# A decode-attention kernel on one core: the last item's keys and values with reversed rows, and 512 columns of its values in loads of their own

## The chip, the cores and the metric

The kernel runs on one core of a Trainium2 chip. The metric is device time in microseconds of one execution; the median of three runs before the change is 695.87 us (695.85 to 696.24). A profiled execution of the same kernel, 695.97 us, is the source of every row shown.

## The reference

Two branches are mixed by a gate. Branch A is one decode step of attention with a cache of 4096 keys, 2 batches, 32 heads of 128; branch B is a feed-forward layer with SiLU.

```
q = (x @ wq) per head
scores = einsum("bhqd,bhkd->bhqk", q, k_cache) * Dh**-0.5
p = softmax(scores); o = einsum("bhqk,bhkd->bhqd", p, v_cache)
a = o.reshape(B, 1, H*Dh) @ wo
b = silu(x @ w1) @ w2
g = sigmoid((x * gate_w).sum(-1)); out = g * a + (1 - g) * b
```

Everything is float32. Keys and values are 134 MB each, and each of their bytes is used once. The softmax sums over all keys of a head, so the order in which a head's keys stand does not matter as long as its values stand in the same order.

## The kernel before

Work goes by items. An item is a group of four heads of one batch; there are 16 (`N`), numbered 0 to 15. Its keys are a run of 2,097,152 numbers that lie one after the other in the cache, and so are its values. `run_of` cuts such a run into 128 rows, one for each partition, of 16384 numbers (64 KB). Head q of the four fills partitions 32q to 32q+31, and a partition holds 128 keys of 128 numbers.

Three slabs of 64 KB per partition lie in SBUF. Keys go to slab `a` (even items) or `b` (odd items) by `load_k`, values to slab `v` by `load_v`; only the values of item 15 go to slab `a`, which the keys of item 14 have left by then. After the last values the weights of the output, `wo`, come in five loads (`load_wo`), the first ones into slab `v`, the last three into slab `b`.

For an item, POOL (L707) and DVE (L713) multiply the keys by the query in place, DVE adds them up to scores (L723) and finds the largest (L731 to L741), ACT takes the exponentials into `pz` (L752), PE multiplies them with the values (L799, 64 matmuls), and a short chain of DVE and PE turns the result into a column of `oP`. At the end PE multiplies `oP` by `wo`: three groups in halves (L590), a merge (L602, L607), and the last group in quarters (L620). The copy of L929 and one small store end the kernel.

All loads are issued by SP, in the order of the program, each when its slab is free, and run on one DMA queue. The loop over items issues the values of item i right after the products of item i, and the keys of item i+2 after the scores of item i. The keys of item 15 therefore stand behind the values of item 13, the values of items 14 and 15 one behind the other, and `wo` behind these. A small planner (`Flow`) notes for every operation which earlier ones it depends on, and turns that into semaphore waits; `dma` takes a semaphore and the value it will have reached (`count`), and `users` lists the operations that last wrote or read a slab. PE's loop covers the items 0 to 14; the matmuls of item 15 (L799) wait for the load of its values by name.

Of the kernel before, what the change touches and what calls it, by code (L numbers as in the profile page):

```python
# [189 lines left out]
def gated_decode(nc, x, kc, vc, wq, wo, w1, w2, gate, out):  # L190
    P = 128
    B, H, SK, DH = kc.shape
# [12 lines left out]
    SLAB = C * DH  # L205
# [11 lines left out]
    N = len(items)  # L217
# [3 lines left out]
    f = Flow(nc)  # L221
# [11 lines left out]
    slab = {n: slabs[:, k * SLAB : (k + 1) * SLAB] for k, n in enumerate("vba")}  # L233

    def part(n, *ks):
        return [f"{n}.{k}" for k in (ks or range(8))]
# [59 lines left out]

    def run_of(flat, i):
        hq, b = items[i]
        return flat[b, hq].rearrange("(p c) -> p c", p=P)

    def load_k(i):
        n = kslab(i)
        f.dma("SP", slab[n], run_of(kflat, i), writes=part(n), count=(h_k[i % 2], 16 * (i // 2 + 1)))
# [3 lines left out]
    def load_v(i):  # L307
        src = run_of(vflat, i)
        if i < N - 1:
            v_load[i] = f.dma("SP", slab["v"], src, writes=part("v"), signal=h_v if i < LOOPED else None)  # L310
            return
        f.dma("SP", slab["a"], src, writes=part("a"))

    def load_wo(g):

# [24 lines left out]
        writes=part("v", 0),  # L340
# [10 lines left out]
        writes=["ident"],  # L351
# [12 lines left out]
        writes=["block"],  # L364
# [7 lines left out]
        writes=["fold"],  # L372
# [5 lines left out]
        writes=["sel"],  # L378
# [5 lines left out]
        writes=["half"],  # L384
# [10 lines left out]
        writes=["pick"],  # L395
# [5 lines left out]
        writes=["own"],  # L401
# [5 lines left out]
        writes=["side"],  # L407
# [7 lines left out]
        writes=["spread"],  # L415
# [5 lines left out]
        writes=["mask"],  # L421
    )
    f.op("DVE", lambda: V.memset(join, 0.0), writes=["join"])
    for e in range(2):
# [7 lines left out]
            writes=["join"],  # L432
        )
        for t in (at, at + 32):
# [4 lines left out]
                writes=["join"],  # L439
# [11 lines left out]
        writes=["xt"],  # L451
# [6 lines left out]
        writes=["gx"],  # L458
# [7 lines left out]
    for b in range(B):  # L466
        for j in range(J):
# [13 lines left out]
                writes=[f"hsum{b}"],  # L481
            )

    def mm_hr():
# [19 lines left out]
        writes=["ps_o"],  # L504
# [7 lines left out]
        writes=["g"],  # L512
# [5 lines left out]
        writes=["gc"],  # L518
# [7 lines left out]
    for e in range(2):  # L526
# [4 lines left out]
            writes=[f"spaced{e}"],  # L531
# [9 lines left out]
        writes=["he"],  # L541
    )
    for e in range(2):
# [6 lines left out]
            writes=[f"seq{e}"],  # L550
# [125 lines left out]
    for u in range(2):  # L676
        for b in range(B):
# [8 lines left out]
                writes=[f"qall{u}{b}"],  # L686
            )

    load_v(0)
    load_k(1)  # L690
    query(0)
# [195 lines left out]
    for i in range(N + 1):  # L887
# [13 lines left out]
        if 1 <= i < N:  # L901
            load_v(i)
# [86 lines left out]
```

## Time and profile before

| | |
|---|---|
| median of three runs | 695.87 us |
| profiled execution | 695.97 us |
| its span (first to last instruction) | 694.6 us |
| busy share of DVE, POOL, PE | 73%, 38%, 31% |
| data moved | 298.32 MB, 429 GB/s over the span |
| share of the 16 DMA engines, data queue | 99.3% |
| one load of keys or values | 8.39 MB |

The page gives the busy time of each engine, the span in 40 slices with the share of the 16 DMA engines, the DMA queues, and the chain of work that ended last. A stretch is a piece of the span for which the same numbers are given; its DMA share counts each packet's duration in the stretch in which the packet began, so in a very short stretch it can pass 1. "SPq" is an issue of a transfer, not its movement.

### The profile page before, as it was taken

How to read it: one execution, taken by the hardware profiler on the slowest of the kernel's cores; microseconds unless marked ns; L12 is line 12 of the kernel's file. 1: busy time of each engine (PE TensorE's matmuls, PEld its weight loads, DVE VectorE, ACT ScalarE, POOL GpSimd, SP SyncE). 2: the span in 40 equal slices, each digit the busy share in tenths (PEclk: the TensorE clock that was granted, in tenths of full speed). 3: DMA queues.
4: the chain of work that ended last, by engine and by line, in shares of the span. 5: the costliest groups of instructions: out<-in, count | busy, mean ns of one | idle time of the engine just before them, and what ended most of it. 6: DMA issues, size and time to landing. Idle time of an engine off the chain costs nothing. (4 is left out here: it accounts for less than half of the span.)

```text
span 694.6 us, 3767 instructions
## 1 busy us (share of the span) xinstructions
PE 211.9 (31%) x1440; PEld 70.2 (10%) x1440; DVE 506.9 (73%) x269; ACT 40.0 (6%) x152; POOL 265.6 (38%) x26
## 2 busy tenths in 40 slices
PE   0073033151331506060412305060513215060556
PEld 0031010010110101010100101010101001010112
DVE  3910958898989697886959596986959595977901
ACT  0001010101010101010010101010000101010100
POOL 1000908190827090815335180906244270907100
PEclk9997556565565657566575757575665757575779
DMA  9999999999999999999999999999999999999997
GB/s 383 429 426 473 426 423 427 423 464 434 423 430 423 442 457 423 423 430 434 464 423 423 430 426 468 426 423 430 423 468 430 423 430 423 453 445 423 430 417 309
DMA packets 6051, 298.32 MB, mean 429 GB/s; under 512 B 652, under 2 KB 672, under 8 KB 928
## 3 DMA queue, kind: packets, MB, share of 16 engines
q1 hardware_dynamic: 6048, 298.27, 99.3%
q8 instruction: 3, 0.05, 0.0%
HBM read 298.26 MB, written 0.01 MB: 429 GB/s over the span
## 5 line engine op out<-in xcount | busy, mean ns | idle before, releaser
L707 POOL TENSOR_TENSOR slabs<-slabs,qsb 128x7680 f32<-128x7680 f32 x16 | 262.4, 16400 | 378.9 <-DMA slabs<-in_A_k_cache_dram 330.8
L723 DVE TENSOR_REDUCE s<-slabs 128x68 f32<-128x8704 f32 (+1 forms) x32 | 276.3, 8677 | 0.0
L799 PE MATMUL ps<-slabs,pz 128*32 128x512 f32 x1024 | 147.2, 739 | 337.1 <-PEq L156 328.9
L713 DVE TENSOR_TENSOR slabs<-slabs,ps 128x8704 f32<-128x8704 f32 x16 | 147.5, 9221 | 103.8 <-DMA slabs<-in_A_k_cache_dram 103.2
L799 PEld LDWEIGHTS ps<-slabs,pz 128*32 128x32 f32 x1024 | 39.7, 132 | 433.5 <-issue 425.2
L752 ACT ACTIVATE pz<-s,nb 32x128 f32<-32x128 f32 x64 | 25.5, 398 | 545.8 <-PE ps L799 353.2
L837 PE MATMUL ps<-osb,pick 128*128 128x512 f32 x32 | 21.1, 747 | 60.9 <-PEq L156 59.9
L821 DVE SCALAR_TENSOR_TENSOR osb<-ps,rg,own 128x512 f32<-128x512 f32 x16 | 12.0, 750 | 23.4 <-PE ps L799 23.1
L852 DVE TENSOR_REDUCE row<-ps 64x128 f32<-64x512 f32 x16 | 10.9, 682 | 24.0 <-PE ps L837 24.0
L773 PE MATMUL ps<-rs,fold 128*128 128x1 f32 x32 | 6.2, 262 | 40.9 <-PEq L156 40.8
L475 DVE SCALAR_TENSOR_TENSOR slabs<-slabs 128x1728 f32<-128x1728 f32 x8 | 16.2, 2019 | 0.3
L487 PE MATMUL ps<-slabs,xz_col 128*32 128x432 f32 x16 | 3.1, 927 | 33.4 <-DVE slabs L475 33.4
L837 PEld LDWEIGHTS ps<-osb,pick 128*128 128x128 f32 x32 | 5.4, 211 | 75.0 <-issue 73.1
L752 ACT ACTIVATION_READ_ACCUMULATOR pz<-s,nb 32x1 f32 x64 | 11.8, 184 | 0.0
L773 PEld LDWEIGHTS ps<-rs,fold 128*128 128x128 f32 x32 | 6.2, 226 | 54.2 <-issue 53.3
L859 DVE STREAM_TRANSPOSE ps<-row 64x256 f32<-64x256 f32 x16 | 10.3, 643 | 0.6
L567 PE MATMUL ps<-slabs,seq 128*32 128x320 f32 x54 | 9.2, 496 | 3.7 <-DVE seq L546 3.7
L642 PE MATMUL ps<-slabs,xz_col 128*32 128x512 f32 x80 | 9.8, 593 | 0.0
L652 PE MATMUL ps<-qall,spread 128*128 (+1 forms) x32 | 9.0, 371 | 0.8 <-ACT qall L680 0.8
L929 DVE COPY slabs<-ps 128x160 f32<-128x160 f32 x1 | 0.3, 324 | 11.9 <-PE ps L620 11.9
L590 PE MATMUL ps<-slabs,oP_xs 128*32 128x320 f32 x96 | 6.9, 434 | 2.4 <-DMA slabs<-in_A_wo_dram 2.4
L652 PEld LDWEIGHTS ps<-qall,spread 128*128 128x128 f32 x32 | 6.1, 236 | 1.7 <-ACT qall L680 1.7
(63 smaller groups left out, 69.8 us busy)
## 6 DMA issues: line engine op xcount, KB each, us to landing
slabs<-in_A_wq_dram SPq DMA_DIRECT2D x1, 10240.0 KB, 44.5
slabs<-in_B_w_dram SPq DMA_DIRECT2D x2, 4320.0 KB, 16.9
slabs<-in_A_wo_dram SPq DMA_DIRECT2D x1, 5120.0 KB, 22.7
slabs<-in_A_wo_dram SPq DMA_DIRECT2D x1, 2560.0 KB, 28.3
slabs<-in_A_wo_dram SPq DMA_DIRECT2D x1, 1600.0 KB, 31.9
slabs<-in_A_wo_dram SPq DMA_DIRECT2D x1, 640.0 KB, 32.9
slabs<-in_A_wo_dram SPq DMA_DIRECT2D x1, 320.0 KB, 33.2
slabs<-in_A_k_cache_dram SPq DMA_DIRECT2D x16, 47.9
```

The lines of the kernel that those rows point to most:

```text
L475: lambda b=b, j=j, at=at: V.scalar_tensor_tensor(hsum[:, b, :], w1t[:, j, :], at, hsum[:, b, :], op0=ALU.mult, op1=ALU.add)
L652: return T_.matmul(ps_q[:, :DH], spread, qall.rearrange("p n b u d -> p (n b u) d")[:, i, :], start=True, stop=True,)
L707: lambda: G_.tensor_mul(k[:, CV:, :], k[:, CV:, :], qsb[:, None, :].to_broadcast([P, C - CV, DH])),
L713: lambda: V.tensor_mul(k[:, :CV, :], k[:, :CV, :], ps_q[:, None, :DH].to_broadcast([P, CV, DH])),
L723: lambda c0=c0, c1=c1: V.reduce_sum(Ss[i % 2][:, c0:c1], k[:, c0:c1, :], axis=AX.X),
L752: last = S_.activation(pz[lo:hi, :, 4 * q : 4 * q + 4], s[lo:hi].rearrange("p (g c) -> p g c", c=4), AF.Exp, bias=nb[lo:hi], scale=SCALE, ...
L773: lambda *_: T_.matmul(ps_t[:, :1], fold.rearrange("p a q c -> p (a q c)"), rs, start=True, stop=True),
L799: last = T_.matmul(ps_v[32 * q : 32 * q + 32, :], pz[:, gr, :], v[:, gr, :], start=(gr < 4), stop=(gr >= NG - 4),)
L821: lambda: V.scalar_tensor_tensor(osb, ps_v.rearrange("p (c d) -> p c d", d=DH), rg, own[:, :, None].to_broadcast([P, 4, DH]), op0=ALU.mult ...
L837: lambda *_: T_.matmul(ps_o, pick, osb.rearrange("p c d -> p (c d)"), start=True, stop=True),
L852: lambda: V.reduce_sum(row, ps_o[:64].rearrange("p (c d) -> p d c", d=DH), axis=AX.X),
L859: lambda: V.transpose(oT.rearrange("p n (e i) -> p n e i", e=2), twice),
```

## The change

For item 15 alone, `run_of` no longer gives 128 rows but 16 blocks of 8 rows, the rows of each block in reversed order: partition 8a+m gets row 8a+7-m. Both its keys and its values go through `run_of`, so their rows stay together, and a block lies within one head. The rows are as long as before.

The values of item 15 are loaded in three transfers in place of one. The first brings columns 0 to 15871 to all 128 partitions. The second brings the last 512 columns (2 KB per partition) to partitions 0 to 95, which are blocks 0 to 11; the third brings these columns to partitions 96 to 127, blocks 12 to 15. All three wait for the same users of slab `a` and count up one new semaphore, to 16, 32 and 48; the matmuls of item 15 wait for 48. Bytes, arithmetic and the order of the issues are otherwise unchanged.

```diff
     def run_of(flat, i):
         hq, b = items[i]
+        if i == N - 1:
+            return flat[b, hq].rearrange("(a m c) -> a m c", a=16, m=8)[:, ::-1, :]
         return flat[b, hq].rearrange("(p c) -> p c", p=P)
 
@@ load_v
-        f.dma("SP", slab["a"], src, writes=part("a"))
+        to, cut, after, last = slab["a"], SLAB - 4 * DH, f.users(part("a")), f.sem("last_values")
+        f.dma("SP", to[:, :cut], src[:, :, :cut], after=after, count=(last, 16))
+        f.dma("SP", to[:96, cut:], src[:12, :, cut:], after=after, count=(last, 32))
+        f.dma("SP", to[96:, cut:], src[12:, :, cut:], writes=part("a"), after=after, count=(last, 48))
```

## The prediction

> **What bounds the kernel now.** I read the head of the page first: busy time of the engines, the two DMA rows of the 40 slices, and the queues.
>
> ```profile
> span 694.6 us, 3767 instructions
> ...
> PE 211.9 (31%) x1440; PEld 70.2 (10%) x1440; DVE 506.9 (73%) x269; ACT 40.0 (6%) x152; POOL 265.6 (38%) x26
> ...
> DMA  9999999999999999999999999999999999999997
> GB/s 383 429 426 473 426 423 427 423 464 434 423 430 423 442 457 423 423 430 434 464 423 423 430 426 468 426 423 430 423 468 430 423 430 423 453 445 423 430 417 309
> DMA packets 6051, 298.32 MB, mean 429 GB/s; under 512 B 652, under 2 KB 672, under 8 KB 928
> ...
> q1 hardware_dynamic: 6048, 298.27, 99.3%
> q8 instruction: 3, 0.05, 0.0%
> ```
>
> One queue keeps all 16 DMA engines busy for 99.3% of the span, while no compute engine passes 73%. The kernel is a stream of 298 MB; whatever makes the engines move a byte more slowly is paid in full, and a transfer can be hidden behind nothing. The timeline's rows of the last items show the order of that stream.
>
> ```profile
> 580.65 0.33 SPq L72 DMA_DIRECT2D slabs<-in_A_v_cache_dram  x1
> ...
> 581.02 0.43 SPq L72 DMA_DIRECT2D slabs<-in_A_k_cache_dram  x1
> ...
> 590.21 9.22 DVE L713 TENSOR_TENSOR slabs<-slabs,ps 128x8704 f32<-128x8704 f32 x1 [5.53 <-DMA slabs<-in_A_k_cache_dram]
> ...
> 618.77 0.80 SPq L72 DMA_DIRECT2D slabs<-in_A_v_cache_dram  x2
> ...
> 628.86 9.22 DVE L713 TENSOR_TENSOR slabs<-slabs,ps 128x8704 f32<-128x8704 f32 x1 [6.07 <-DMA slabs<-in_A_k_cache_dram]
> ...
> 656.84 2.31 SPq L72 DMA_DIRECT2D slabs<-in_A_wo_dram  x5
> ...
> 667.50 9.16 PE L799 MATMUL ps<-slabs,pz 128*32 128x512 f32 x64 [8.15 <-DMA slabs<-in_A_v_cache_dram]
> ```
>
> The keys of item 15 (the last) are issued at 581.02, behind the values of item 13, and are used from 628.86. The values of items 14 and 15 are issued together at 618.77; those of item 15 are used from 667.50. So the stream after 609.5 is: keys 15, values 14, values 15, then the five loads of wo. The stretches of 19.3 us give their rates (third number from the end the granted clock, then DMA share, GB/s).
>
> ```profile
> 590.20:609.50 19.30, 0.00 (x0) 0.00 (x0) 19.16 (x5) 0.00 (x0) 16.39 (x1) 0.50 1.00 435
> 609.50:628.80 19.30, 10.86 (x70) 3.28 (x70) 10.92 (x10) 2.22 (x9) 0.00 (x0) 0.77 1.00 435
> 628.80:648.10 19.30, 0.00 (x0) 0.00 (x0) 19.09 (x5) 0.00 (x0) 16.39 (x1) 0.50 1.00 435
> 648.10:667.40 19.30, 10.04 (x68) 2.99 (x68) 11.30 (x12) 1.96 (x8) 0.00 (x0) 0.77 0.98 426
> 667.40:679.50 12.10, 10.29 (x66) 2.49 (x66) 1.44 (x3) 0.00 (x0) 0.00 (x0) 0.82 1.00 432
> ```
>
> Every load of 8.39 MB takes 19.3 us: 435 GB/s, or 27.2 GB/s for each of 16 engines, so an engine's eight rows of 64 KB take 2.41 us each. The chain that ended last, in order of time, shows the end.
>
> ```profile
> 657.78 31.89 DMA slabs<-in_A_wo_dram
> 689.67 0.14 issue
> 689.80 2.16 PE ps L620 x56
> 691.97 0.02 issue
> 691.99 0.51 PE ps L620 x8
> 692.50 0.02 issue
> 692.52 0.32 DVE slabs L929
> ```
>
> The landings of wo end the kernel, with 2.9 us of matmuls, copy and issue behind the third-last of them. How the 16 engines finish is in quarter-microsecond stretches.
>
> ```profile
> 689.75:690.00 0.25, 0.20 (x8) 0.22 (x12) 0.00 (x0) 0.00 (x0) 0.00 (x0) 1.00 0.84 338
> 690.00:690.25 0.25, 0.25 (x16) 0.24 (x12) 0.00 (x0) 0.00 (x0) 0.00 (x0) 1.00 0.39 154
> ...
> 691.50:691.75 0.25, 0.25 (x16) 0.12 (x4) 0.00 (x0) 0.00 (x0) 0.00 (x0) 1.00 0.00 0
> 690.25:691.50 1.25, 1.25 (x43) 1.01 (x36) 0.00 (x0) 0.00 (x0) 0.00 (x0) 1.00 0.18 74
> ```
>
> Most engines have moved their last byte by 690.25, but from there to 691.50 a share of 0.18, or 0.18 x 16 = 2.9 engines, is still at work. Three engines are some 1.3 us late. The trace does not name them. The queue of instructions moved three packets; one falls in this stretch of 1 us:
>
> ```profile
> q1 hardware_dynamic: 34, 0.42, 99.4%
> q8 instruction: 1, 0.02, 5.9%
> ```
>
> 5.9% of 16 engine-microseconds is 0.95 us on one engine. Three packets, three late engines: I take it that each packet set one engine back for the rest of the run.
>
> **The change, part by part.** Part 1, fewer bytes for the last engines. Which transfer runs on how many engines shows in the packets under 512 B, which hold each engine's completion write: 652 = 40 x 16 + 3 x 4. Forty transfers have 128 rows; the three others (x, gate, output) have a slowest dimension of four on one side, though x fills eight partitions. So I expect the load of twelve blocks on 12 engines and that of four blocks on 4. The 512 columns are 512/16384 = 1/32 of the load, 19.3/32 = 0.60 us per engine. The last four engines get none of them (-0.60), the first four get two shares (+0.60 and some packet overhead, say +0.7), the middle eight stay. If the late three are among the last four, the end moves from 691.9 by -0.6; the first four, 1.3 us ahead, stay covered. If they are elsewhere it moves by 0 to +0.7. The tail of PE follows the landings either way.
>
> The Trainium skill, page "DMA: Bandwidth & Descriptors", section "Why a DMA increments its semaphore by 16 and not by 1", says that the engine count is the largest number up to 16 that divides the slowest dimensions of both sides, on the lowest-numbered engines; the 652 agree.
>
> Part 2, three issues for one. The row of 618.77 gives 0.80 us for two, so 0.8 more on SP. Nothing is behind them on SP until wo at 656.84, 38 us later, and the queue is fed 29 us ahead (618.77 against 648.1). Cost nothing; without that cover 0.8. The matmuls of L799 wait for all three, as for the one before. The two small loads' 128 extra packets lie in the shares above.
>
> Part 3, the source in sixteen blocks of eight rows, read backwards. This applies to all of keys 15 and values 15, 16.5 MB. No load of the trace has this form, so I bound it. From below: a row stays one piece of 64 KB (62 KB for the values), and the rate stays 435 GB/s as in the stretches above: 0. A gain has a reason against it, since each engine already streams without a gap (share 1.00). From above: the sixteen engines need not meet the partitions as they do now. If engine e takes block e, neighbouring partitions in one engine, two engines can want the same way into SBUF at a time, and two that share a way get half the rate each. Then keys 15 take 2 x 19.3, +19.3; values 15 without the 512 columns 2 x 18.7, +18.7; together +38.0. The nearest row to such sharing is the packet of instructions: 16 KB beside a data stream on one engine took 0.95 us, where 27.2 GB/s would give 0.60.
>
> Which end? The 128-row form lets the hardware deal out single rows, the new one only blocks of eight; what the old dealing bought is then lost, and the engines of a pair start these loads within 1.3 us of each other, against 9.7 us for four rows, so they would meet nearly all the time. I take the upper end, though the choice is close.
>
> The Trainium skill, page "SBUF — State Buffer", section "Door 1: The DMA port swizzle", gives each of 16 ports two groups of four partitions 32 apart and 27.2 GB/s, and "DMA: Bandwidth & Descriptors", section "The descriptor swizzle", says that a 128-partition transfer deals the partitions so that each engine has one port. By these rules blocks 0 and 4 would both be in port 0, then both in port 2, and half the ports would idle: the sum would be +38. If the swizzle held for the new form too, it would be part 1 alone. No row here shows which.
>
> Sum: 695.97 (the profiled execution; its span of 694.6 and 1.4 around it) + 19.3 + 18.7 + 0 for part 1 (between -0.6 and +1.2, since the pieces may share too) = 734.0. The median of the runs is 0.1 below the profiled one: **733.9**. All that waits on the keys of item 15 (L713, L707, the exponentials, the issue of wo) moves 19.3 with them; wo, issued 10.6 us ahead of need now (656.84 against 667.4), would be issued 29 us ahead, so no new gap opens.
>
> **The rivals.** *Same rate, late engines relieved* (the other side): the layout costs nothing and part 1 alone remains. For it: 64 KB rows, share 1.00, 16 engines on both forms. Against: the dealing out must change. Time 695.87 - 0.6 = 695.3 where the late engines are the last four, up to 696.6 where one is among the first; it decides where the keys of item 15 still land by 629. This holds the case that the small loads spread over all 16 engines after all: 695.9.
>
> *Sharing only once*: the engines of a pair drift apart by four rows in the keys of item 15, because one is served first, and then no longer meet. That costs four rows, 4 x 2.41 = 9.7 us once: 705.6; partial overlap fills the space up to 733.9. For it: engines run independently, as the late ones show. Against: a lateness of 1.3 us persists here and does not grow.
>
> *A layout that gains over 0.2%*: it needs 1.4 us, more than the 1.3 that all three late engines have. Against it everything above.
>
> **How the numbers follow.** Half rate in both loads 0.44, sharing in part 0.14, same rate 0.40, gain 0.02. 0.2% (1.4 us) is what a measurement of this kernel can tell from no change; the same-rate rival lies wholly inside it. So slower 0.58, same 0.40, faster 0.02. Predicted 733.9; its own range with partial sharing is 704 to 736. Since the cases of both signs hold nearly all the chance, the range runs from 694.9 to 736.
>
> **What would show it.** In the changed kernel's stretches, 609.5 to 648.1 at about 217 GB/s and the values of item 15 likewise, with the values of item 14 between at 435; L713's last wait longer by 19.3 us; wo landing some 38 us later, the tail behind it as now. Packets: 128 + 16 more, 668 under 512 B if the small loads run on 12 and 4 engines (652 - 16 + 32). Wrong would be: keys 15 landing by 629 (then the same-rate rival, and the tail from 690.25 to 691.50 shortens by 0.6), or a slow first load and a fast second (sharing once).

## The result and the profile after

The median of six runs is 741.45 us (740.52 to 742.49), against 696.02 us before (695.81 to 696.72): a ratio of 1.0652, interval 1.0638 to 1.0665. That is 45.4 us slower. The forecast was 733.9, with a range up to 736: the direction and the mechanism came out, the size did not. Lines of the code have moved by five, so L718 answers to L713 of before, L804 to L799, L625 to L620 and L934 to L929.

The head of the page of the changed kernel:

```profile
span 740.2 us, 3769 instructions
...
DMA  9999999999999999999999999999999999899897
GB/s 385 443 441 439 414 447 432 425 446 429 429 446 418 439 446 414 443 443 418 443 439 418 446 439 411 450 443 411 446 446 411 446 397 220 184 393 259 185 313 324
DMA packets 6195, 298.32 MB, mean 403 GB/s; under 512 B 668, under 2 KB 688, under 8 KB 1072
...
q1 hardware_dynamic: 6192, 298.27, 99.4%
q8 instruction: 3, 0.05, 0.0%
```

The same 298.32 MB, and the DMA engines are as busy as before (99.4%). What has changed is the row of GB/s: two dents near the end, to about half. An engine with a slow packet counts as busy, so the share (99.3% before) does not show the loss. The packets under 512 B are 668, which is 652 - 16 + 32: this fits pieces on 12 and 4 engines, as forecast.

The timeline of the changed kernel, at the uses of the last loads:

```profile
612.53 8.49 PE L804 MATMUL ps<-slabs,pz 128*32 128x512 f32 x64 [29.86 <-PEq L156]
...
652.49 9.22 DVE L718 TENSOR_TENSOR slabs<-slabs,ps 128x8704 f32<-128x8704 f32 x1 [27.38 <-DMA slabs<-in_A_k_cache_dram]
...
674.91 9.72 PE L804 MATMUL ps<-slabs,pz 128*32 128x512 f32 x64 [50.94 <-PEq L156]
...
684.69 2.31 SPq L72 DMA_DIRECT2D slabs<-in_A_wo_dram  x5
...
713.57 9.17 PE L804 MATMUL ps<-slabs,pz 128*32 128x512 f32 x64 [26.38 <-DMA slabs<-in_A_v_cache_dram]
```

The rows of before that answer to the first and the third of these, from the same view:

```profile
609.63 9.08 PE L799 MATMUL ps<-slabs,pz 128*32 128x512 f32 x64 [26.09 <-PEq L156]
...
648.23 8.56 PE L799 MATMUL ps<-slabs,pz 128*32 128x512 f32 x64 [26.57 <-PEq L156]
```

The keys of item 15 come 23.6 us later (652.49 for 628.86) and its values 46.1 us later (713.57 for 667.50). The plain loads beside them are late too: the values of item 13, which stand ahead of these keys, by 2.9 us (612.53 for 609.63), and those of item 14 by 26.7 us (674.91 for 648.23), 3.1 more than the keys ahead of them. The issue of wo follows at 684.69, 29 us ahead of its turn.

The chain that ended last, in order of time:

```profile
685.63 49.57 DMA slabs<-in_A_wo_dram
735.20 0.14 issue
735.34 2.19 PE ps L625 x56
737.53 0.03 issue
737.56 0.51 PE ps L625 x8
738.08 0.02 issue
738.10 0.33 DVE slabs L934
```

It is the chain of before, 45.6 us later (738.10 for 692.52), with the same tail behind the landings.

How long a row takes shows in the queue's share of a stretch: share x 16 engines x length, over the packets. This is the queue's row of the changed kernel in the stretch 612.2 to 642.8 (keys of item 15).

```profile
DMA packets 97, 6.36 MB, mean 208 GB/s; under 512 B 0, under 2 KB 0, under 8 KB 0
...
q1 hardware_dynamic: 97, 6.36, 100.3%
```

100.3% x 16 x 30.6 / 97 = 5.06 us for a row of 64 KB. The same view of the kernel before, 609.5 to 628.8:

```profile
DMA packets 144, 8.39 MB, mean 435 GB/s; under 512 B 16, under 2 KB 16, under 8 KB 16
...
q1 hardware_dynamic: 144, 8.39, 100.3%
```

Here 16 of the 144 are completion writes; 100.3% x 16 x 19.3 / 128 = 2.42 us. And the changed kernel from 675 to 705 (values of item 15, rows of 62 KB):

```profile
DMA packets 97, 6.16 MB, mean 205 GB/s; under 512 B 0, under 2 KB 0, under 8 KB 0
...
q1 hardware_dynamic: 97, 6.16, 99.3%
```

99.3% x 16 x 30 / 97 = 4.91 us. So both loads run slowly from end to end; a row takes 2.1 times as long.

### The profile page after: what moved, and what is told of

Same layout as the page of the kernel before. It is cut to its first block, busy times and chain, and to the rows that moved or that the text cites. A ratio compares the mean times of both kernels' runs of the same rounds, so it can differ in the third digit from the quotient of the medians.

```text
span 740.2 us, 3769 instructions
## 1 busy us (share of the span) xinstructions
PE 212.1 (29%) x1440; PEld 70.1 (9%) x1440; DVE 506.9 (68%) x269; ACT 40.0 (5%) x152; POOL 265.6 (36%) x26
## 2 busy tenths in 40 slices
DMA packets 6195, 298.32 MB, mean 403 GB/s; under 512 B 668, under 2 KB 688, under 8 KB 1072
## 3 DMA queue, kind: packets, MB, share of 16 engines
q1 hardware_dynamic: 6192, 298.27, 99.4%
## 5 line engine op out<-in xcount | busy, mean ns | idle before, releaser
L804 PE MATMUL ps<-slabs,pz 128*32 128x512 f32 x1024 | 147.3, 740 | 382.0 <-PEq L156 355.7
L718 DVE TENSOR_TENSOR slabs<-slabs,ps 128x8704 f32<-128x8704 f32 x16 | 147.5, 9221 | 124.7 <-DMA slabs<-in_A_k_cache_dram 124.1
L804 PEld LDWEIGHTS ps<-slabs,pz 128*32 128x32 f32 x1024 | 39.9, 133 | 478.2 <-issue 451.7
L934 DVE COPY slabs<-ps 128x160 f32<-128x160 f32 x1 | 0.3, 325 | 11.3 <-PE ps L625 11.3
```

The lines of the kernel that those rows point to most:

```text
L718: lambda: V.tensor_mul(k[:, :CV, :], k[:, :CV, :], ps_q[:, None, :DH].to_broadcast([P, CV, DH])),
L804: last = T_.matmul(ps_v[32 * q : 32 * q + 32, :], pz[:, gr, :], v[:, gr, :], start=(gr < 4), stop=(gr >= NG - 4),)
```

## The experiments

Three theories could make these rows. A: blocks of eight partitions go to an engine whole, and two engines share a way into SBUF, that is, whatever limits how fast a group of partitions can be written. B: reading rows backwards is slow. C: the sixteen engines now read places 512 KB apart in HBM, and these collide there. No row of the profile names the partitions that an engine writes, so A is judged by the times that follow from it. In all of the runs the values of item 15 are one load unless the edit says otherwise, and of longer edits only the lines that matter are shown. Where a kernel ran once there is no interval; for effects of 20 us and more that is enough.

**Blocks of four.** Reversal kept, blocks halved:

```diff
-            return flat[b, hq].rearrange("(a m c) -> a m c", a=16, m=8)[:, ::-1, :]
+            return flat[b, hq].rearrange("(a m c) -> a m c", a=32, m=4)[:, ::-1, :]
```

> Item 15's keys and values in 32 blocks of four rows, each block reversed, in place of 16 blocks of eight; its values in one load. The bytes and the backward step are those of the changed kernel. Theory A (two engines share a way into SBUF because blocks of eight partitions are dealt out whole): four neighbouring partitions already go to one engine in the plain load if the rule of the Trainium skill (page DMA: Bandwidth & Descriptors, section The descriptor swizzle) holds, so this can be dealt out as before: 696, and 435 GB/s in both loads. Theory B (reading rows backwards is slow): 741, and 205 GB/s as in the changed kernel. Theory C (the sixteen streams stand 512 KB apart in HBM): they stand 256 KB apart here as before, 696.

Measured 695.84 us (before, on the same chip, 695.90). Its stretch of the keys of item 15:

```profile
609.50:628.80 19.30, 10.24 (x70) 3.20 (x70) 10.91 (x10) 2.23 (x9) 0.00 (x0) 0.77 1.00 435
```

Full rate with every row read backwards: B falls. The Trainium skill (page "DMA: Bandwidth & Descriptors", section "The descriptor swizzle") has four neighbouring partitions on one engine in the plain load; that blocks of four cost nothing and blocks of eight do agrees.

**Blocks forward, spaced.** Blocks of eight kept, reversal and the 512 KB taken away (the item then computes on other data):

```diff
+        if i == N - 1:
+            gap = 8 * SLAB + 8 * DH
+            start = B * H * SK * DH - 15 * gap - 8 * SLAB
+            return type(flat)(flat.tensor, start, [[gap, 16], [SLAB, 8], [1, SLAB]])
```

> Item 15's keys and values in 16 blocks of eight rows, rows in forward order, the blocks 516 KB apart in HBM in place of 512 (so they reach over the neighbouring heads, and item 15 computes on other data); values in one load. Theory A: dealt out in blocks of eight as in the changed kernel, 741 and 205 GB/s in both loads. Theory B: no backward step, 696. Theory C: no streams 512 KB apart, 696.

Measured 742.55 us. The stretch of its keys, 612.2 to 642.8:

```profile
612.20:642.80 30.60, 11.69 (x70) 3.45 (x70) 8.32 (x10) 2.23 (x9) 0.00 (x0) 0.67 1.02 210
```

As slow as the changed kernel, without a backward row and without the distance of 512 KB.

**Every other row.** The counterpart: plain dealing, rows 128 KB apart, so that engines stand 512 KB apart (again other data):

```diff
+        if i == N - 1:
+            return flat.rearrange("b g c -> (b g c)")[-2 * P * SLAB :].rearrange("(p t c) -> p t c", p=P, t=2)[:, 0, :]
```

> The kernel before, only that the 128 rows of item 15's keys and values are every other row of a stretch twice as long (rows 128 KB apart in place of 64, so item 15 computes on other data). By the plain dealing of four neighbouring partitions to one engine the streams then stand 512 KB apart, as in the changed kernel. Theory A and B: 696, 435 GB/s. Theory C: 741, 205 GB/s in both loads.

Measured 695.84 us, and the keys' stretch reads as before:

```profile
609.50:628.80 19.30, 11.28 (x70) 3.33 (x70) 10.87 (x11) 2.23 (x9) 0.04 (x1) 0.77 1.00 435
```

C falls. What matters is the size of the block.

**Halves.** Sharing made on purpose, in the kernel before, with no blocks at all:

```diff
-        f.dma("SP", slab["a"], src, writes=part("a"))
+        after, last = f.users(part("a")), f.sem("last_values")
+        f.dma("SP", slab["a"][:64], src[:64], after=after, count=(last, 16))
+        f.dma("SP", slab["a"][64:], src[64:], writes=part("a"), after=after, count=(last, 32))
```

> The kernel before, only that the values of item 15 come as two plain loads, partitions 0 to 63 and then 64 to 127. Nothing is reversed, no blocks. By the Trainium skill (page SBUF - State Buffer, section Door 1: The DMA port swizzle) each load then reaches 8 of 16 ports. Theory A: two engines share a way in all along, so the load takes 38.6 us at exactly half rate (696 + 19.3 = 715) or some 41 us if the 205 GB/s of the changed kernel is what sharing gives (717). Theories B and C: 696.

Measured 719.94 us, 24.0 more than before and 3 above the 717 that was expected with the low rate. The queue's row in its stretch 650.4 to 681.0:

```profile
DMA packets 113, 6.36 MB, mean 208 GB/s; under 512 B 16, under 2 KB 16, under 8 KB 16
...
q1 hardware_dynamic: 113, 6.36, 101.0%
```

97 data packets, 101.0% x 16 x 30.6 / 97 = 5.10 us each: the row time of the changed kernel, from nothing but a smaller span of partitions. So A holds, and 2.1 times is what sharing costs, not something special to blocks. The Trainium skill (page "SBUF — State Buffer", section "Door 1: The DMA port swizzle") gives 64 partitions 8 of 16 ports and at most about 218 GB/s, 196 measured at 1 MiB; 208 lies between. That the thing shared is that page's port is its reading; the runs show a way in that two engines cannot both fill.

**Eighths.** Eight plain loads of 16 partitions for the values of item 15:

```diff
-        f.dma("SP", slab["a"], src, writes=part("a"))
+        after, last = f.users(part("a")), f.sem("last_values")
+        for k in range(8):
+            rows, w_ = slice(16 * k, 16 * k + 16), part("a") if k == 7 else ()
+            f.dma("SP", slab["a"][rows], src[rows], writes=w_, after=after, count=(last, 16 * k + 16))
```

> The kernel before, only that the values of item 15 come in eight plain loads of 16 partitions each. By the Trainium skill (page SBUF - State Buffer, section Door 1: The DMA port swizzle) 16 partitions reach 4 of 16 ports, so four engines share one. Sharing by ports: 4 ports at the 25.7 GB/s that a shared one gave is 103 GB/s, 8.39 MB take 81.6 us in place of 19.3: 758 to 762. If sharing costs half at most however many meet: 717 to 720. If small partition counts cost nothing: 696.

Measured 752.12 us, and from 655 to 715:

```profile
655.00:715.00 60.00, 8.37 (x64) 2.39 (x56) 4.46 (x12) 1.96 (x8) 0.00 (x0) 0.59 0.97 113
```

About a quarter of 435 GB/s where 16 partitions are written at a time. The rate falls further with fewer partitions, though not in proportion: an eighth of the partitions keeps a quarter of the rate, as the expectation had it, so the loss does not stop at half. The time is 6 us below the expectation, since I had carried the low rate of the pairs over, and 113 GB/s is a little more than a quarter. Engines at the seam of two loads may already reach the next partitions; that is not shown.

**Keys alone.** Only the keys of item 15 in blocks (its values then stand in another order than the weights):

```diff
-        if i == N - 1:
+        if i == N - 1 and flat is kflat:
```

> Only the keys of item 15 in reversed blocks of eight; its values plain and in one load (so values meet the weights of other keys inside each block of eight). Theory A: one shared load of two, rows of 5.1 us in place of 2.4, 8 x 2.7 = 21.4 and some 2 us for the late engines at its two borders: 718 to 720, like the halves. If the engines of a pair drift apart in the first load and no longer meet in the second: nearly all of the 45 us, above 735.

Measured 718.93 us, +23.0: about half of the loss belongs to each load, and the pairs do not drift apart for the second one. The rows account for 8 x (5.06 - 2.42) = 21.1 of it.

**One load of values.** The changed kernel without the pieces:

```diff
-        f.dma("SP", to[:, :cut], src[:, :, :cut], after=after, count=(last, 16))
-        f.dma("SP", to[:96, cut:], src[:12, :, cut:], after=after, count=(last, 32))
-        f.dma("SP", to[96:, cut:], src[12:, :, cut:], writes=part("a"), after=after, count=(last, 48))
+        f.dma("SP", slab["a"], src, writes=part("a"))
```

> The changed kernel with the values of item 15 in one load again (blocks of eight, reversed, kept). Theory A (the blocks alone make the loss): 741.5, with both loads at 205 GB/s; taking the pieces away gives back their own sharing, about 1 us at most, and costs the 0.6 us of relief for the last four engines. If the pieces carry part of the loss: clearly less, below 739.

Measured 742.48 us (739.97 to 744.28), ratio 1.0655, interval 1.0636 to 1.0673. The pieces make no difference that these runs can tell; the blocks alone make the loss.

**The pieces by themselves.** Four kernels give the pieces without blocks of eight in the large loads. The first two keep reversed blocks of eight in the last 512 columns of keys and values only, all else plain; they differ in the values' load.

```diff
 # keys: the main columns plain, then
+            tail.append(f.dma("SP", slab[n][:, cut:], blocks_of(kflat, i)[:, :, cut:], after=after))
 # values: the main columns plain, then, on 12 and 4 engines
+        f.dma("SP", to[:96, cut:], back[:12, :, cut:], after=after, count=(last, 32))
+        f.dma("SP", to[96:, cut:], back[12:, :, cut:], writes=part("a"), after=after, count=(last, 48))
 # or, in the second kernel, on all 16
+        f.dma("SP", to[:, cut:], back[:, :, cut:], writes=part("a"), after=after, count=(last, 32))
```

> Only the last 512 columns of item 15's keys and values stand in reversed blocks of eight: the keys' in one load of 128 partitions, the values' in loads of 96 and 32; all other columns plain. Theory A with the three late engines among the last four: the keys' 512 columns cost at most 0.7 us (0.60 us of load at half rate), the values' pieces take 0.6 us from the late engines and bring 0.6 to 1.3 to the first four: 695.3 to 696.3, below e8_tail_even by some 0.6. If the late engines are not among the last four: above e8_tail_even.

> As e7_tail_columns, but the values' 512 columns in one load of 128 partitions on all 16 engines: no engine gets fewer bytes. Two pieces of 0.60 us at half rate: 696.0 to 697.3. The difference to e7_tail_columns is the relief of the last four engines alone.

Measured 697.95 us for the pieces on 12 and 4 engines (ratio 1.0028, interval 1.0017 to 1.0038) and 697.80 for the even one (1.0024, 1.0014 to 1.0033), before 695.96. Both are slower by 0.2 to 0.3%, both lie above what was expected (up to 696.3 and up to 697.3), and the relief makes no difference. The other two use blocks of four throughout, which deal out freely:

```diff
 # values, on 12 and 8 engines
+        f.dma("SP", to[:96, cut:], src[:24, :, cut:], after=after, count=(last, 32))
+        f.dma("SP", to[96:, cut:], src[24:, :, cut:], writes=part("a"), after=after, count=(last, 48))
 # or, in the second kernel, on all 16
+        f.dma("SP", to[:, cut:], src[:, :, cut:], writes=part("a"), after=after, count=(last, 32))
```

> The changed kernel with blocks of four in place of blocks of eight: keys, values and the pieces of 96 and 32 partitions as before otherwise. The large loads are then dealt out as e1_blocks_of_four showed (no cost). The pieces are 24 and 8 blocks, so by the rule of the Trainium skill (page DMA: Bandwidth & Descriptors, section Why a DMA increments its semaphore by 16 and not by 1) they run on 12 and 8 engines: the last four engines get 0.60 us less, the first eight 0.30 us more. If the late engines are among the last four and the small pieces share little: 695.4, below e10_four_even by 0.4 to 0.6. If the pieces' sharing eats it, as in e7_tail_columns: 696 to 697.

> As e9_four_pieces, but the 512 columns come in one load on all 16 engines, dealt out like the large ones: neither sharing nor relief. 696.0, the same as before.

Measured 697.01 us (ratio 1.0012, interval 1.0003 to 1.0021) and 696.00 us (0.9997, 0.9988 to 1.0006), before 696.23. The first has 672 packets under 512 B, which is 652 - 16 + 16 + 12 + 8 and fits pieces on 12 and 8 engines. How the engines finish in the kernel with the even load:

```profile
690.25:691.50 1.25, 1.25 (x42) 0.98 (x36) 0.00 (x0) 0.00 (x0) 0.00 (x0) 1.00 0.19 76
690.25:690.50 0.25, 0.25 (x16) 0.24 (x10) 0.00 (x0) 0.00 (x0) 0.00 (x0) 1.00 0.33 133
690.50:690.75 0.25, 0.25 (x16) 0.24 (x9) 0.00 (x0) 0.00 (x0) 0.00 (x0) 1.00 0.16 61
```

And in the kernel with the pieces:

```profile
690.25:691.50 1.25, 1.25 (x44) 1.01 (x36) 0.00 (x0) 0.00 (x0) 0.00 (x0) 1.00 0.52 205
690.25:690.50 0.25, 0.25 (x17) 0.24 (x8) 0.00 (x0) 0.00 (x0) 0.00 (x0) 1.00 0.82 328
690.50:690.75 0.25, 0.25 (x16) 0.25 (x8) 0.00 (x0) 0.00 (x0) 0.00 (x0) 1.00 0.93 369
```

With the even load three engines (0.19 x 16) work on alone, as before the change; with the pieces nearly all work until 690.75. The bytes did move, and to the right engines as far as they were behind by then. By the start and length of each packet in the trace, the last rows of the large load end between 664.95 and 665.42 on fourteen engines of the kernel with the pieces, at 666.62 and 666.91 on the two late ones, and from 666.57 to 667.00 no packet of 2 KB begins any more:

```profile
DMA packets 6, 0.06 MB, mean 143 GB/s; under 512 B 3, under 2 KB 3, under 8 KB 3
```

All 128 packets of the pieces had begun before, so neither late engine carried one. But at 690.7 all 16 engines still have data to move, where with the even load only three have, and the last bytes land at nearly the same time (691.6 and 691.7): what the many now do longer uses up what the few are spared. This profiled run took 696.02 us, one of the three shortest of its eleven; where the other 1.0 us of the median goes it does not show. No version beat the kernel before; blocks of four with the even load equal it.

## Why the prediction was wrong

**Part 3, the layout of the two loads.** The mechanism was right: pairs of engines share a way in for the whole of both loads, in the keys and again in the values, so "sharing only once" and "same rate" are out. The step that failed is the term of the sum, "two that share a way get half the rate each". The prediction took exact half as the upper end; a pair together reaches 2 x 64 KB in 5.06 us, 25.9 GB/s in place of 27.1. The keys then cost 8 x (5.06 - 2.42) = 21.1, not 19.3, and the values, whose 62 KB rows would take 2.34 alone, 8 x (4.91 - 2.34) = 20.6, not 18.7: 41.7 in place of 38.0, which alone leads out of the range (695.9 + 41.7 = 737.6).

The reason for choosing this end was right only in part. It was that the old form deals out single rows, and that what this bought is lost when whole blocks are dealt out; but blocks of four lost nothing (695.84), and only blocks of eight do. The prediction called the choice close, and that the direction came out is partly luck.

**No term for the borders.** The remaining 3.7 of 45.4 us had no term in the prediction at all. The rows place it where the loads meet: the values of item 13 and of item 14, plain loads both, lose 2.9 and 3.1 us of their own (612.53 and 674.91, above). These can't be added to the 41.7, since from use to use the two slow loads add only 20.7 and 19.4. The queue's rows of the changed kernel show two things there. From 605.9 to 606.8, four engines that are behind the others begin their last row of item 13's values:

```profile
DMA packets 4, 0.26 MB, mean 291 GB/s; under 512 B 0, under 2 KB 0, under 8 KB 0
...
q1 hardware_dynamic: 4, 0.26, 96.6%
```

96.6% x 16 x 0.9 / 4 = 3.48 us each, where a row of this plain load takes 2.42. The other twelve engines began the blocks of the keys from 607.5 on, while these rows were still moving. A load that nobody changed is thus slowed by what the other engines do, which is sharing seen between two loads. From 647.8 to 652.1, each of the 16 engines begins its first row of item 14's values:

```profile
DMA packets 32, 1.05 MB, mean 244 GB/s; under 512 B 16, under 2 KB 16, under 8 KB 16
...
q1 hardware_dynamic: 32, 1.05, 92.0%
```

92.0% x 16 x 4.3 / 16 = 3.96 us, of which 0.02 is the completion write: on average 1.5 us more than 2.42, though the load is plain again; the 16 packets took 2.75 to 4.64 each. So a slow load still weighs on the row behind it; why is not shown. The run with the keys alone has 23.0 - 21.1 = 1.9 left over, for two borders instead of four. How the rest divides stays open, since single runs of the changed kernel differ by up to 2 us and those of the one without pieces by up to 4.

**Part 1, the relief.** The engine counts were right (668). The gain of 0.6 was not there: with the dealing free, the pieces made the kernel 0.12% slower than before and the even load left it the same. The two engines that were late by then were relieved, but the pieces cost the others as much. Nor could all three be relieved knowingly: the third packet of instructions begins at 684.48 in the kernel before, 17 us after the values are in (667.4), so by the prediction's own reading the third engine falls behind only then. The tail behind the landing at 689.67 is 3.2 us by the rows of the chain (to 692.84), not 2.9; the sum does not use it.

**Part 2, the issues.** Three issues on SP cost nothing, as worked out: the chain of waits has no step of theirs.

**The chances.** 0.58 for slower held; the range stopped at 736 because its upper end was the half-rate sum with some 2 us on top, and nothing in it stood for a rate below half. An end taken from an ideal ratio is not a bound.

## What to carry to other kernels

In a kernel that streams, look at the GB/s of a stretch, not at the DMA share: the share stayed at 99.4% while two loads ran at half speed. Before cutting a load's rows into blocks, ask how many partitions one engine then takes in a row: blocks of four were free here and blocks of eight doubled the time of the load. To move a few bytes from one DMA engine to another, price the sharing of the small pieces too; here it cost as much as the move gained.

## What the runs showed that was not expected

A pair of engines on one way loses 4 to 5% beyond the half (25.9 GB/s of 27.1), alike in blocks (5.06 us) and in plain halves (5.10 us). A very small block load is dear for its size: 512 columns of keys and values in blocks of eight, 1/32 of two loads, cost 1.8 us in all (697.80 against 695.96), where double time on 0.60 us twice would be 1.2.
